# Feed-forward in two halves of its inner units, with partial sums in DRAM

## The chip, the cores and the metric

One Trainium2 chip, one core. The metric is the device time of one execution in microseconds (us). Engines are called PE (TensorE, matrix products), PEld (its weight loads), DVE (VectorE), ACT (ScalarE), POOL (GpSimd) and SP (SyncE, which here only issues DMAs).

## The reference

Sparse attention, then a mixture of experts with one expert per token, then a dense feed-forward; all results in float32.

```python
scores = scale * (q @ k.T)                        # 4 batches, 8 heads, 576 x 576, head size 64
scores = where(scores >= rowmax - tau, scores, -1e9)
x = softmax(scores) @ v                           # 2304 tokens of 512 numbers
e = argmax(normalized x @ normalized expert_emb)  # 8 experts, inner size 1024
x = gate * (relu(x @ w1[e]) @ w2[e])
h = x @ w_in                                      # 512 -> 2048
out = (h * tanh(softplus(h))) @ w_out             # 2048 -> 512
```

The feed-forward's weights w_in and w_out come as 64-bit floats (512 KB for a piece of 128x512 numbers) and have to be narrowed to 32 bits on the chip.

## The kernel before

Every matrix product of the experts and the feed-forward is made of three: both operands are split into a rounded high part (a cast on ACT) and the remainder (a subtraction on DVE or POOL), and PE multiplies high by high, high by low and low by high.

A planner (`Plan`, from line 85) holds a list of operations, each with its engine, an assumed duration, what it reads and writes, a priority and a phase, and writes out one fixed order for every engine. Buffers are rings: `Handle` objects take their places in the order of a number `at`. The numbers `PR` and `PR2` (lines 37 and 38) are the priorities' offsets. Phase 0 is everything up to the last expert; phases 1 to 15 are branches for tokens that overflow an expert's room (none run here); phase 16 is what comes after them. An engine passes the branch only when its part of phase 0 is done.

Stages: attention (to about 300 us, lines 460 to 606), experts (about 320 to 556 us), feed-forward (556 us to the end). In the experts' stage `visit` (line 987) handles one expert: SP loads four 1 MB weight chunks, each chunk is split in two halves by `weight_part` (lines 961 and 963; `PR2['split']` names, for each of the eight halves, the engine of the cast and that of the subtraction), POOL gathers the expert's tokens (line 969) and scales them (line 972), PE transposes them into a PSUM pair (line 1040), multiplies by w1 (line 1064); ACT and DVE free the PSUM pair (lines 1069 and 1070); PE multiplies by w2 (line 1087), ACT copies to `osb` (line 984) and SP stores it to `y_dram`. PSUM has three pairs of banks ("S") and two single banks ("B").

During that stage `narrow_late` (line 1232) narrows all 32 pieces of w_in and w_out: `ffn_narrow` (line 1211) loads a piece to `fraw` (two buffers), ACT scales the exponent word (line 1221), DVE does three integer operations (lines 1224, 1225, 1228), and SP stores the float32 piece to DRAM. `ffn_weights` (line 1242) loads it back later, in four chunks (c = 0 to 3, each for 4 of 16 blocks of 128 inner units), and splits it (lines 1256 and 1260). Chunks 2 and 3 use the experts' weight buffers `wh` and `wl`.

The feed-forward takes its 18 token tiles of 128 in groups of 2, 4, 4, 4, 4 (`GROUPS`). For a group `ffn_rows` (line 1262) loads the transposed rows and splits them (lines 1290 and 1292); `ffn` (line 1296) runs units of one inner block of 128 (two for the group of 2 tiles): 12 matmuls per block into a PSUM bank (line 1329), tanh and two more ACT passes (1337 to 1339), a reciprocal and a product on DVE (1343, 1344), the split of the result (ACT 1347, POOL 1348), and three matmuls for each tile into that tile's sum (line 1355), which stays in PSUM, in two pairs, over all 16 blocks. At the end of a group ACT takes each sum out (line 1361) and POOL scatters it to the output (line 1365). The first `SOON` = 5 units of the first group belong to phase 0.

## Time and profile before

| | |
|---|---|
| median of three runs (all) | 972.65 us (971.48 to 973.35) |
| the profiled execution, its span | 974.42 us, 972.7 us |
| PE busy | 912.6 us (94%) |
| DVE busy | 742.2 us (76%) |
| ACT busy | 557.7 us (57%) |
| POOL busy | 353.8 us (36%) |
| DMA | 115.47 MB, mean 119 GB/s |

The span runs from the first to the last instruction. A busy PE is one with a matmul in flight; its rate also depends on the granted clock. The stages differ much in what is busy, so the table of stages in the next section but one is the view to start from.

### The profile page before, as it was taken

The numbers are of one execution on the slowest core, as the hardware profiler recorded it, in microseconds if no ns is written. First come the engines' busy times: TensorE is split into PE (matmuls) and PEld (weight loads), VectorE is DVE, ScalarE is ACT, GpSimd is POOL, SyncE is SP. The second block draws the span as 40 slices with busy tenths as digits, with TensorE's granted clock in tenths as the row PEclk, the third lists the DMA queues.
The fourth block names the chain that finished last, engine by engine and source line by source line (L and its number), as shares of the span: only waits on it lengthen the run. The fifth ranks groups of instructions, "written<-read, shape, count | busy, mean of one in ns | idle before, by whom it ended". The sixth has DMA issues, their size and how long they took to land. (4 is left out here: it accounts for less than half of the span.)

```text
span 972.7 us, 17476 instructions
## 1 busy us (share of the span) xinstructions
PE 912.6 (94%) x6574; PEld 727.2 (75%) x6574; DVE 742.2 (76%) x1032; ACT 557.7 (57%) x916; POOL 353.8 (36%) x445
## 2 busy tenths in 40 slices
PE   5899999998989999988899998999999999999997
PEld 3556565555557899888899986888888878888885
DVE  6898988888847477967898885992958596586972
ACT  3688887787766454554566763652644445363551
POOL 4233333433223544434323732423432333333333
PEclk9899999999999999998999999999999999999999
DMA  4123433323243788989889631001010001000001
GB/s 154 60 75 103 122 104 108 96 82 112 77 153 117 286 284 303 323 255 331 301 307 325 219 113 46 23 0 44 22 42 3 22 1 44 1 1 22 22 1 44
DMA packets 45637, 115.47 MB, mean 119 GB/s; under 512 B 11029, under 2 KB 16170, under 8 KB 41450
## 3 DMA queue, kind: packets, MB, share of 16 engines
q1 hardware_dynamic: 42426, 104.03, 31.8%
q0 software_dynamic: 3120, 10.25, 3.1%
q8 instruction: 54, 0.88, 0.4%
q14 instruction: 37, 0.30, 0.1%
HBM read 91.55 MB, written 22.70 MB: 117 GB/s over the span
## 5 line engine op out<-in xcount | busy, mean ns | idle before, releaser
L1343 DVE RECIPROCAL p<-p 128x512 f32<-128x512 f32 x72 | 241.0, 3347 | 100.7 <-ACT p L1339 100.7
L1348 POOL TENSOR_TENSOR lo<-p,hi 128x512 fp32r<-128x512 f32 x72 | 93.0, 1293 | 177.4 <-ACT hi L1347 100.8
L514 PE MATMUL D<-QK 64*128 64x288 f32 (+1 forms) x640 | 109.0, 465 | 19.3 <-DVE P L521 8.3
L520 ACT ACTIVATE E<-D,m 128x576 f32<-128x576 f32 x144 | 104.1, 743 | 36.7 <-DVE m L518 31.5
L518 DVE TENSOR_REDUCE m<-D 128x1 f32<-128x576 f32 x144 | 104.7, 752 | 18.6 <-PE D L514 18.4
L521 DVE SCALAR_TENSOR_TENSOR P<-D,thr,E 128x576 f32<-128x576 f32 x128 | 101.5, 813 | 15.1 <-ACT E L520 14.2
L541 ACT COPY T<-D 128x1024 f32<-128x1024 f32 (+1 forms) x80 | 74.3, 930 | 31.5 <-PE D L538 30.8
L519 POOL TENSOR_SCALAR thr<-m,ntau 128x1 f32<-128x1 f32 x144 | 38.7, 271 | 136.0 <-DVE m L518 118.2
L572 PE MATMUL D<-T,V 128*64 128x512 f32 x320 | 84.7, 615 | 0.9 <-DVE P L521 0.5
L1347 ACT CAST hi<-p 128x512 fp32r<-128x512 f32 x72 | 43.9, 610 | 70.1 <-PE S L1355 32.2
L514 PEld LDWEIGHTS D<-QK 64*128 64x128 f32 (+1 forms) x640 | 48.5, 186 | 44.4 <-issue 19.1
L963 DVE TENSOR_TENSOR wl<-raw,wh 128x1024 fp32r<-128x1024 f32 x49 | 69.5, 1445 | 12.1 <-ACT wh L961 12.0
L1087 PE MATMUL B<-lo,wh 128*128 128x240 f32 (+6 forms) x256 | 75.6, 295 | 1.7 <-DVE lo L1070 1.7
L1087 PE MATMUL B<-hi,wh 128*128 128x240 f32 (+6 forms) x256 | 75.6, 295 | 1.1 <-ACT osb L984 1.1
L1064 PE MATMUL S<-xh,wh 128*128 128x240 f32 (+6 forms) x256 | 75.9, 296 | 0.3 <-DVE lo L1070 0.3
L1087 PE MATMUL B<-hi,wl 128*128 128x240 f32 (+6 forms) x256 | 75.3, 294 | 0.0
L1064 PE MATMUL S<-xl,wh 128*128 128x240 f32 (+6 forms) x256 | 75.2, 294 | 0.0
L1064 PE MATMUL S<-xh,wl 128*128 128x240 f32 (+6 forms) x256 | 75.1, 293 | 0.0
L963 POOL TENSOR_TENSOR wl<-raw,wh 128x1024 fp32r<-128x1024 f32 x15 | 38.1, 2541 | 84.8 <-ACT wh L961 78.3
L961 ACT CAST wh<-raw 128x1024 fp32r<-128x1024 f32 x64 | 63.4, 1050 | 2.7 <-PE B L1087 2.6
L1337 ACT ACTIVATE p<-S 128x512 f32<-128x512 f32 x36 | 21.5, 598 | 64.9 <-PE S L1329 49.8
L572 PEld LDWEIGHTS D<-TL,V 128*64 128x64 f32 x320 | 23.7, 139 | 46.2 <-issue 46.0
(298 smaller groups left out, 2340.1 us busy)
## 6 DMA issues: line engine op xcount, KB each, us to landing
raw<-in_wm_dram SPq DMA_DIRECT2D x32, 1024.0 KB
QK<-in_qk_dram SPq DMA_DIRECT2D x32, 432.0 KB
V<-in_v_dram SPq DMA_DIRECT2D x16, 512.0 KB
fraw<-in_w_in_dram SPq DMA_DIRECT2D x16, 512.0 KB
fraw<-in_w_out_dram SPq DMA_DIRECT2D x16, 512.0 KB
x_dram<-xs SPq DMA_DIRECT2D x16, 256.0 KB
w_in_dram<-c SPq DMA_DIRECT2D x16, 256.0 KB
w_out_dram<-c SPq DMA_DIRECT2D x16, 256.0 KB
```

What stands on the lines that cost most here:

```text
L514: nc.tensor.matmul(o, lhsT=QK()[r, a, q0:q0 + w], rhs=QK()[r, a, S:], start=True, stop=True)
L518: add("DVE", 680, lambda: nc.vector.tensor_reduce(m(), sv(), axis=AX.XY, op=ALU.max, negate=True), r=[sc], w=[m], prio=at + PR["max"])
L520: add("ACT", 660, lambda: nc.scalar.activation(Ev(), sv(), AF.Exp, bias=m(), scale=1.0), r=[sc, m], w=[E], prio=at + PR["exp"])
L521: add("DVE", 750, lambda: nc.vector.scalar_tensor_tensor(outs[0]().rearrange("p (a b) -> p a b", a=2), sv(), thr(), Ev(), op0=ALU.is_ge, o ...
L541: add("ACT", (2 * w + 100) / 1.2, lambda: nc.scalar.copy(T()[:, :, 0:w], pt()[:, :, 0:w]), r=[pt], w=[T], prio=at + PR["Tc"])
L572: mul = lambda j, o, c, rhs: nc.tensor.matmul(o, lhsT=V1()[:, c, :], rhs=rhs, start=(a == 0), stop=(a == 4))
L961: add("ACT", t_act(1024, False), lambda: nc.scalar.copy(hi()[:, s], raw()[:, s]), r=[kr], w=[kh], prio=prio, fill=fill)
L963: add(le, d, lambda: e.tensor_tensor(lo()[:, s], raw()[:, s], hi()[:, s].bitcast(F32), op=ALU.subtract), r=[kr, kh], w=[kl], prio=prio + . ...
L1064: hd(nc.tensor.matmul(hp(), lhsT=a()[:, kc, f], rhs=x()[:, kc, cols], start=(i == 0), stop=(i == 11)))
L1087: nc.tensor.matmul(o()[:, 0:N_], lhsT=w[a]()[:, u % 4, 128 * d:128 * (d + 1)], rhs=H2[x], start=(u == 0 and i == 0), stop=(u == 7 and i == 2))
L1343: v.reciprocal(q_(), q_())
L1348: add("POOL", t_pool(512), lambda q_=q_, gh=gh, gl=gl: g.tensor_tensor(gl(), q_(), gh().bitcast(F32), op=ALU.subtract), r=[q_, gh], w=[gl] ...
```

## The change

The feed-forward goes through its inner units in two halves. Ten sequences `sq` run: groups 0 to 4 with blocks 0 to 7, then groups 4 to 0 with blocks 8 to 15. The first half's sums are doubled on ACT and stored to a DRAM tensor `part` (18 x 128 x 512); in the second half they are loaded back, and DVE adds them while it takes the sums out of PSUM. The group in the middle keeps its rows; every other group loads and splits its rows again. Groups are 3, 4, 4, 4, 3 tiles; a unit is one block; `SOON` is 4. Rows of sequences 1 and 3 lie in the experts' weight buffers.

Of the 32 weight pieces 20 (`16 + EXTRA`) are narrowed in the experts' stage as before. The other twelve, chunk 2 of w_out and chunk 3 of both, are narrowed in the feed-forward's first half, split from there straight into their place (`direct`), and make no trip through DRAM. Narrowing works in place: the first DVE operation is a shift by a constant that overwrites the loaded words, and the last overwrites ACT's result; the buffers `c` go, and there are four of `b`.

Besides, the half `split[5]` (chunk 2, second half) of the experts' weights is subtracted on DVE instead of POOL, the second expert's tokens are scaled on ACT, the planner assumes longer DMA times (y stores 6000 for 2000 ns, expert weights 7500 for 2000, and others), and most numbers of `PR` and `PR2` are different, those of attention too.

```diff
-GROUPS = (2, 4, 4, 4, 4)
-SOON = 5
+GROUPS = (3, 4, 4, 4, 3)
+SOON = 4
+EXTRA = 4
-PR2 = {... 'split': (['ACT', 'DVE'], ['ACT', 'POOL'], ['ACT', 'DVE'], ['ACT', 'DVE'], ['ACT', 'DVE'], ['ACT', 'POOL'], ['ACT', 'DVE'], ['ACT', 'DVE']), 'sl': 28000, ... 'n1': 0.6, ...}
+PR2 = {... 'split': (('ACT', 'DVE'), ('ACT', 'POOL'), ('ACT', 'DVE'), ('ACT', 'DVE'), ('ACT', 'DVE'), ('ACT', 'DVE'), ('ACT', 'DVE'), ('ACT', 'DVE')), 'sl': 2000, ... 'n1': 0.48, ... 'dx': 15.1, 'dp': 278.01, 'd_pool': (0, 1, 2, 3), ...}
...
+        self.part = dr.tile([18, 128, 512], F32, name="part")
...
-            self.fetch(self.ids[:, j:j + 1], self.x_dram[:, :], need, xg, -600 + T + 10 * k, "POOL" if v else "ACT")
+            self.fetch(self.ids[:, j:j + 1], self.x_dram[:, :], need, xg, -600 + T + 10 * k, "POOL" if v > 1 else "ACT")
...
-            v.tensor_tensor(w(), words(U32, 0), self.by29.to_broadcast([128, 512]), op=ALU.logical_shift_right)
-            v.scalar_tensor_tensor(w(), words(U32, 1), 0x80000000, w(), op0=ALU.bitwise_and, op1=ALU.bitwise_or)
-        add("DVE", 690, lambda: v.scalar_tensor_tensor(w(), e().bitcast(U32), 3, w(), op0=ALU.logical_shift_left, op1=ALU.bitwise_or), r=[ke], w=[kw], prio=at)
+        add("DVE", 560, lambda: v.tensor_scalar(words(U32, 0), words(U32, 0), 29, None, op0=ALU.logical_shift_right), r=[kr], w=[kt], prio=at)
+        add("DVE", 690, lambda: v.scalar_tensor_tensor(words(U32, 0), words(U32, 1), 0x80000000, words(U32, 0), op0=ALU.bitwise_and, op1=ALU.bitwise_or), r=[kr, kt], w=[kt], prio=at)
+        add("DVE", 690, lambda: v.scalar_tensor_tensor(e().bitcast(U32), e().bitcast(U32), 3, words(U32, 0), op0=ALU.logical_shift_left, op1=ALU.bitwise_or), r=[kt, ke], w=[ke], prio=at)
...
-        for x, (n, i) in enumerate(self.pieces):
+        for x, (n, i) in enumerate(self.pieces[:16 + EXTRA]):
...
+            x = self.pieces.index((n, 4 * c + q))
+            direct = x >= 16 + EXTRA and self.io[n].dtype != F32
+            self.pl.phase = 0 if c < 2 else OVER + 1
+            if direct:
+                z = x - 16
+                bt = 501 + 100 * z / 16 + R["dx"]
+                raw, e = h("f", "fraw", [128, 2 * YW], F32, 2, bt), h("f", "b", [128, 512], F32, 4, bt)
+                self.ffn_narrow(n, 4 * c + q, bt + R["dp"], lambda dt, raw=raw: raw()[:, 0:1024].bitcast(dt), e, [raw, e], store=False)
+                add("ACT", t_act(512, False), lambda s=s, e=e: nc.scalar.copy(hi()[:, s], e()), r=[e], w=[(th, q)], prio=bt + R["dp"])
+                eng, dur, d = ("POOL", t_pool(512), g) if q in R["d_pool"] else ("DVE", t_dve(512), v)
+                add(eng, dur, lambda s=s, e=e, d=d: d.tensor_tensor(lo()[:, s], e(), hi()[:, s].bitcast(F32), op=ALU.subtract), r=[e, (th, q)], w=[(tl, q)], prio=bt + R["dp"])
+                continue
...
-        have = [("y", -1, k) for k in range(2)] + [("y", v, d) for v in range(2 if gi == 0 else NE) for d in range(4)]
+        have = [("y", -1, k) for k in range(2)] + [("y", v, d) for v in range(3 if sq == 0 else NE) for d in range(4)]
...
+        nu, u0 = 8 // fw, half * 8 // fw
...
+            if not half:
+                add("ACT", t_act(512), lambda ob=ob, t=t: ad(t, nc.scalar.mul(ob()[:, 0:512], acc(t), 2.0)), r=[ak(t)], w=[ob], prio=at + R["ob"])
+                add("SP", 600, lambda ob=ob, t=t: nc.sync.dma_start(self.part[t0 + t], ob()[:, 0:512]), r=[ob], w=[("part", t0 + t)], prio=at, lat=4500, dma=262e3)
+                continue
+            pt = self.row("q32", at + 12 + t)
+            add("SP", 600, lambda pt=pt, t=t: nc.sync.dma_start(pt()[:, 0:512], self.part[t0 + t]), r=[("part", t0 + t)], w=[pt], prio=at + R["fy"] + 5 + t, lat=4500, dma=262e3)
+            add("DVE", t_dve(512), lambda ob=ob, t=t, pt=pt: ad(t, v.scalar_tensor_tensor(ob()[:, 0:512], acc(t), 2.0, pt()[:, 0:512], op0=ALU.mult, op1=ALU.add)), r=[ak(t), pt], w=[ob], prio=at + R["ob"])
...
+        for sq in range(2 * G):
+            half, gi = sq // G, min(sq, 2 * G - 1 - sq)
+            self.pl.phase = OVER + 1 if sq else 0
+            if sq != G:
+                rows = self.ffn_rows(gi, sq)
+            self.ffn(gi, half, sq, rows)
```

## Rows read from the trace of the kernel before

**Rows 1.** Table of stages: stretch, busy us of each engine (instructions), clock, DMA, GB/s
```profile
core 0: us, PE busy (x) PEld busy (x) DVE busy (x) ACT busy (x) POOL busy (x), PEclk, DMA share, GB/s
0.00:300.00 300.00, 272.10 (x3009) 166.52 (x3010) 240.78 (x588) 221.78 (x339) 102.78 (x256) 0.98 0.31 105
352.00:450.00 98.00, 89.42 (x544) 87.65 (x544) 81.24 (x101) 50.15 (x83) 38.79 (x22) 0.97 0.90 300
450.00:556.60 106.60, 100.47 (x861) 99.42 (x861) 91.54 (x112) 66.20 (x125) 45.08 (x24) 0.98 0.86 294
556.60:610.30 53.70, 46.88 (x278) 39.47 (x278) 38.49 (x25) 27.44 (x48) 16.91 (x13) 0.97 0.27 82
610.30:966.10 355.80, 355.36 (x1549) 290.10 (x1547) 255.38 (x130) 167.68 (x283) 120.97 (x113) 1.00 0.06 18
```

**Rows 2.** Waits of PE, 352.0 to 556.6: total us, times, longest us
```profile
PE S L1040 <- issue: 7.2, 4, 4.3
PE S L1040 <- POOL wl L963: 4.4, 2, 2.4
```

**Rows 3.** Timeline of PE: start, us, what [idle before it <- releaser]
```profile
402.44 1.06 PE L1040 MATMUL S<-ident,q 128*128 128x128 f32 x8 [1.36 <-issue]
...
440.47 1.94 PE L1040 MATMUL S<-ident,q 128*128 128x128 f32 x8 [4.33 <-issue]
...
471.91 1.07 PE L1040 MATMUL S<-ident,q 128*128 128x128 f32 x8 [2.44 <-POOL wl L963]
...
496.43 1.06 PE L1040 MATMUL S<-ident,q 128*128 128x128 f32 x8 [1.98 <-POOL wl L963]
```

**Rows 4.** Timeline of DVE, 425 to 445
```profile
436.45 2.83 DVE L1224 TENSOR_TENSOR c<-fraw,by 128x512 uint32<-128x512 uint32 x1
...
439.92 0.45 DVE L1070 SCALAR_TENSOR_TENSOR lo<-S,hi 128x288 fp32r<-128x288 f32 x1
```

**Rows 5.** All narrowing operations by line: count, then ns least/median/most, first and last start
```profile
L1224 DVE TENSOR_TENSOR c<-fraw,by x32: 674/684/2829, 345.2 to 526.9; 128x512 uint32<-128x512 uint32 x32
L1225 DVE SCALAR_TENSOR_TENSOR c<-fraw,c x32: 691/693/2783, 346.3 to 527.6; 128x512 uint32<-128x512 uint32 x32
```

**Rows 6.** Timeline of POOL, 395 to 530
```profile
397.78 2.50 POOL L963 TENSOR_TENSOR wl<-raw,wh 128x1024 fp32r<-128x1024 f32 x1 [6.54 <-DMA raw<-in_wm_dram]
...
435.88 2.85 POOL L963 TENSOR_TENSOR wl<-raw,wh 128x1024 fp32r<-128x1024 f32 x1 [5.20 <-ACT wh L961]
...
468.22 2.73 POOL L963 TENSOR_TENSOR wl<-raw,wh 128x1024 fp32r<-128x1024 f32 x1 [5.19 <-ACT wh L961]
...
492.86 2.60 POOL L963 TENSOR_TENSOR wl<-raw,wh 128x1024 fp32r<-128x1024 f32 x1 [3.80 <-ACT wh L961]
```

**Rows 7.** Stretches, line 1224 alone: DVE busy us (instructions), clock, DMA, GB/s
```profile
352.00:450.00 98.00, 13.79 (x17) 0.97 0.90 300
450.00:530.00 80.00, 12.60 (x13) 0.98 0.90 312
```

**Rows 8.** The page's costliest groups: count | busy us, mean ns | idle before, releaser
```profile
L963 DVE TENSOR_TENSOR wl<-raw,wh 128x1024 fp32r<-128x1024 f32 x49 | 69.5, 1445 | 12.1 <-ACT wh L961 12.0
...
L963 POOL TENSOR_TENSOR wl<-raw,wh 128x1024 fp32r<-128x1024 f32 x15 | 38.1, 2541 | 84.8 <-ACT wh L961 78.3
```

**Rows 9.** Groups by line in the feed-forward, 610.3 to 966.1, columns as above
```profile
L1343 DVE RECIPROCAL p<-p 128x512 f32<-128x512 f32 x65 | 217.5, 3347 | 86.6 <-ACT p L1339 86.6
L1348 POOL TENSOR_TENSOR lo<-p,hi 128x512 fp32r<-128x512 f32 x66 | 85.3, 1294 | 163.9 <-ACT hi L1347 90.1 <-PE S L1355 47.2 <-PE B L1329 11.3
...
L1344 DVE SCALAR_TENSOR_TENSOR p<-p,B 128x512 f32<-128x512 f32 x33 | 22.7, 687 | 1.2
```

**Rows 10.** The chain that ended last: start, us, what
```profile
592.34 3.12 PE S L1329 x24
...
610.46 5.53 PE B L1329 x24
...
966.12 0.61 ACT p L1361
```

**Rows 11.** One seam between groups, columns as in rows 1
```profile
780.00:810.00 30.00, 29.79 (x131) 24.04 (x130) 21.59 (x12) 11.73 (x21) 10.73 (x12) 1.00 0.05 18
```

**Rows 12.** Timeline of DVE, 595 to 605
```profile
601.65 1.62 DVE L1292 TENSOR_TENSOR lo<-fraw,hi 128x512 fp32r<-128x512 f32 x1
603.19 0.68 DVE L1292 TENSOR_TENSOR c<-fraw,b 128x512 fp32r<-128x512 f32 x1
```

More of the change, by code (lines that the diff above doesn't have):

```diff
@@ L1171, in overflow @@
         X, H = h("p32"), [h("p32", 1 + a) for a in range(2)]
-        R = [h("b", 0), h("b", 1), h("c", 0), h("c", 1)]
+        R = [h("b", x) for x in range(4)]
         xg, xp, o, y = h("q32"), h("S"), h("B"), h("osb")
@@ L1285, in ffn_rows, with ffn @@
         for z in range(2):
-            add("SP", 600, lambda z=z: nc.sync.dma_start(raw[z]()[:, 0:2 * w].rearrange("p (x n) -> p x n", x=2), self.y_dram[2 * z:2 * z + 2, :, c0:c0 + w].rearrange("x p n -> p x n")), r=have, w=[raw[z]], prio=at + R["fy"] + z, lat=2000, dma=1024.0 * w)
+            add("SP", 600, lambda z=z: nc.sync.dma_start(raw[z]()[:, 0:2 * w].rearrange("p (x n) -> p x n", x=2), self.y_dram[2 * z:2 * z + 2, :, c0:c0 + w].rearrange("x p n -> p x n")), r=have, w=[raw[z]], prio=at + R["fy"] + z, lat=4500 if sq else 2000, dma=1024.0 * w)
         out = []
         for kc in range(4):
-            hi, lo = (lambda t=t: t().bitcast(F32R)[:, 0:w] for t in X[kc])
+            hi, lo = (lambda i=i, kc=kc: view(i, kc) for i in range(2))
             add("ACT", t_act(w, False), lambda hi=hi, kc=kc: nc.scalar.copy(hi(), part(kc)), r=[raw[kc // 2]], w=[X[kc][0]], prio=at + R["fx"] + kc)
-            eng, dur, e = ("POOL", t_pool(w), g) if gi > 1 or gi and kc % 2 else ("DVE", t_dve(w), v)
+            eng, dur, e = ("POOL", t_pool(w), g) if sq > 1 or sq and kc % 2 else ("DVE", t_dve(w), v)
             add(eng, dur, lambda hi=hi, lo=lo, kc=kc, e=e: e.tensor_tensor(lo(), part(kc), hi().bitcast(F32), op=ALU.subtract), r=[raw[kc // 2], X[kc][0]], w=[X[kc][1]], prio=at + R["fx"] + kc)
             out.append((hi, lo))
-        return X, out, ids
-    def ffn(self, gi, rows):
+        return X, out
+    def ffn(self, gi, half, sq, rows):
         nc, add, h = self.nc, self.pl.add, self.h
@@ L1301, in ffn @@
         fw, w = 4 // nt, 128 * nt
-        at = 500 + 40 * gi
-        Xk, X, ids = rows
-        idu = h("f", "fiu", [128, 4], U32, 2, at + 50)
-        place = lambda u: 409 + .1 * u if gi == 0 and u < SOON else at + 2 * u * fw
-        accs = [self.big(place(R["acc"] + x / 8)) for x in range(nt // 2)]
+        at = 500 + 20 * sq
+        last = sq == 2 * len(GROUPS) - 1
+        Xk, X = rows
+        if half:
+            ids = h("f", "fid", [128, 4], F32, 3, at)
+            add("SP", 600, lambda: nc.sync.dma_start(ids()[:, 0:nt], self.id_dram[128 * t0:128 * (t0 + nt), :].rearrange("(t p) o -> p (t o)", p=128)), w=[ids], prio=at + R["fy"] + 4, lat=2000, dma=20e3, after=[self.last_id])
+            idu = h("f", "fiu", [128, 4], U32, 2, at + 25)
+        nu, u0 = 8 // fw, half * 8 // fw
+        place = lambda u: 409 + .1 * u if sq == 0 and u < SOON else at + 2 * u * fw
+        accs = [self.big(place((R["acc"] if sq else 3.6) + x / 8)) for x in range((nt + 1) // 2)]
         acc = lambda t: accs[t // 2]()[:, t % 2, :]
@@ L1309, in ffn @@
         ad = lambda t, ins: self.of_bank(*ak(t), ins)
-        for u in range(16 // fw):
-            self.pl.phase = 0 if gi == 0 and u < SOON else OVER + 1
-            au, pu = place(u), at + 2.5 * u * fw
+        for x in range(nu):
+            u = u0 + x
+            self.pl.phase = 0 if sq == 0 and x < SOON else OVER + 1
+            au, pu = place(x), at + 2.5 * x * fw
             if u % 4 == 0:
@@ L1354, in mm2 @@
                         for n, (a, x) in enumerate(((gh, wh), (gh, wl), (gl, wh))):
-                            ad(t, nc.tensor.matmul(acc(t), lhsT=a()[:, k], rhs=x, start=(u == 0 and f == 0 and n == 0), stop=(u == 16 // fw - 1 and f == fw - 1 and n == 2)))
-                late = gi == len(GROUPS) - 1 and u >= 16 // fw - 4
+                            ad(t, nc.tensor.matmul(acc(t), lhsT=a()[:, k], rhs=x, start=(u == u0 and f == 0 and n == 0), stop=(u == u0 + nu - 1 and f == fw - 1 and n == 2)))
+                late = last and x >= nu // 2
                 add("PE", 3 * fw * 227, mm2, r=[gh, gl] + keys("w_out"), w=[ak(t)], prio=at + 1100 + 10 * t + .1 * u if late else pu + R["lag"] + .1 * t)
@@ L1414, in feed_forward @@
                 self.ffn_weights(n, c, (400 if c > 1 else 480) + 2 * c + x, tags[2 * c + x])
[L1415 to L1418 removed]
+        G = len(GROUPS)
+        for sq in range(2 * G):
[4 more added lines that the diff above has]
+            self.ffn(gi, half, sq, rows)
     def finish(self):
```

80 lines of the change are left out of this document (38 added, 42 removed).

## The prediction

> **What bounds the kernel now.** I read the stage table first [rows 1]: idle time of TensorE (PE) is the stretch minus its busy time. The feed-forward from 610.30 to 966.10 us leaves 355.80 - 355.36 = 0.4 us of idle PE at full clock: no other engine holds it there. The experts from 352.00 to 556.60 lose (98.00 - 89.42) + (106.60 - 100.47) = 14.7 us, and the granted clock of 0.97 and 0.98 costs about 2.9 + 2.1 = 5.0 us more. The entry into the feed-forward, 556.60 to 610.30, loses 6.8 us and 1.6 us of clock. Attention loses 27.9 us before 300. So what this change can win lies in about 28 us (14.7 + 5.0 + 6.8 + 1.6).
>
> Next, PE's waits in the experts [rows 2]: 7.2 and 4.4 us of 14.7 end at line 1040, the transposes of an expert's gathered rows. The table names POOL or nobody as releaser, so I put the queues side by side at one place. PE's transposes start at 440.47, after 4.33 us of nothing [rows 3]. They need a PSUM pair, which line 1070 frees on VectorE (DVE); there it ends at 439.92 + 0.45 = 440.37, and ahead of it lies a narrowing operation (line 1224) of 2.83 us [rows 4]. The same form has a median of 0.684 us [rows 5]. During just that stretch POOL runs a 2.85 us piece of line 963 [rows 6]. Such a POOL piece, of 2.50 to 2.85 us, starts 3.5 to 4.7 us ahead of each of the four transposes that end a long stop (402.44, 440.47, 471.91, 496.43), and each is its expert's second POOL piece, the one of weight chunk 2. The experts' cause is thus DVE, 83% and 86% busy, stretched by POOL at a bad moment; that the DMA engines are 0.90 and 0.86 busy is the second suspect.
>
> The Trainium skill (GPSIMD Engine Reference, 1. Specifications) says that POOL shares its SBUF interfaces with VectorE and contends with DVE instructions that have two SBUF inputs. The trace agrees, 2.83 us beside 0.684 [rows 4, 5].
>
> **The change, part by part.** Sums are made against the profiled execution's own 974.4 us (span 972.7 and 1.7 around it); the median of the three runs lies 1.8 us lower, and I take that off at the end.
>
> *Experts.* (a) Twelve of 32 narrowings leave: each is three DVE operations; line 1224 takes 13.79 us for 17 before 450 and 12.60 for 13 after it [rows 7], 26.39/30 = 0.88 each, so I take 2.6 us a piece: 31 us of DVE. (b) 12 x (0.5 + 0.25 + 0.25) MB of transfers become 12 x 0.5 MB, and those move to the feed-forward. (c) The POOL piece of chunk 2 goes to DVE: eight pieces of 2.54 us leave POOL, DVE gets eight of at most 1.45 [rows 8], 12 us. It is the piece of every PE stop above. DVE so falls by 19 us net. But pieces run as their buffers allow, 17 of 30 in the first of the two parts; the remaining 20 can fill that part as before, so (a) helps after 450 and (c) everywhere. Without (c)'s collision each of the four stops shortens by up to 2.83 - 0.68 = 2.1 us: 8.6. The clock, which was lost beside these stops, gives back most of its 5.0: I take 3.5. Of the other waits after 450, where 31 us of DVE work thin out, I take 2. Together -14. Bounds: -19 (all of 19.7 but a little) and -4 (half of the 8.2 lost after 450, nothing before). -14 is nearer to what the four pairs of rows show in common.
>
> *Entry.* Before, 16 weight pieces of chunks 2 and 3 are split beside the first units; now they aren't. But the first group has three tiles, and only four units of it can run before the overflow's branch. A unit of 384 columns asks 12 + 9 matmuls of PE and 384/512 of a gate of DVE, 0.75 x (3.35 + 0.69) = 3.0 us [rows 9]; where only the nine second matmuls (2.1 us) are left, DVE sets the pace and PE loses 1 us a unit, three times, and the fill after the branch stays. I take -2, bounds -6 and +4.
>
> *Feed-forward, PE.* The columns are the same: 192 x 2304 for the first product, 48 matmuls per tile for the second. A 512-column matmul takes 5.53/24 = 0.230 us; 24 of 256 columns take 3.12, 0.130 each, above half of it [rows 10]. A 256-column group less can only help: 0, bounds -2 and 0.
>
> *Feed-forward, DVE in the first half.* 24 full gates of 3.347 + 0.687 and 16 of three quarters: 97 + 48 = 145 us; twelve narrowings at 2.6: 31; small splits 2: 178 us, beside PE's half, (192 x 0.130 + 1632 x 0.230)/2 = 200 us [rows 10]. It fits at 89%, where the stage before has 255.38/355.80 = 72%. PE holds four PSUM banks of finished first products, some 11 us of slack of order. Cost +2; bounds 0 and +18 (rival 3).
>
> *Feed-forward, other engines.* Four groups of rows are loaded and split again: 16 casts on ACT and 16 POOL pieces of 1.29 us [rows 9], 21 us on a POOL that is 121 of 356 us busy. Twelve raw loads and 36 tile transfers of 0.25 MB in 400 us lie on a DMA system that is 0.06 busy. On SP's queue these stand in front of later row loads: a raw load waits for one of two raw buffers, and rows, partial sums and token numbers behind it wait too. Rows are asked for about half a group ahead, and a group lasts 8 units of 4.2 to 5.5 us, 33 to 44 us, so nothing. If that cover goes, a late row load stops PE for its landing and split.
>
> *Nine seams instead of four, one of them without new rows.* A seam now costs 30.00 - 29.79 = 0.2 us [rows 11]. In the second half its sums leave PSUM on DVE, behind a reciprocal of 3.35 us, where ACT took 0.61 [rows 10]; the new group's second products wait for that behind first products already in four banks. +2, bounds 0 and +8.
>
> *Tail.* The last eviction is 0.69 on DVE instead of 0.61 on ACT: +0.1, bounds -1 and +2. *Attention.* Its priorities change, its work does not: 0, bounds -4 and +4 of 27.9 idle.
>
> Sum: -14 - 2 + 0 + 2 + 0 + 2 + 0 + 0 = -12; 974.4 - 12 = 962.4; less 1.8 gives 960.6: I say 961.
>
> **The rivals.** *1, all the cover holds:* the experts give 19, the entry 6, DVE and seams cost 1: 974.4 - 24 - 1.8 = 948.6. For it: every long stop has the same moved POOL piece. Against: DVE before 450 keeps as many narrowings, and the other POOL piece (chunk 0) still meets them. Chance 0.20.
>
> *2, the change doesn't do what it says:* the experts wait for DMA and gathers, 20 narrowings keep the part before 450 as dense, and DVE gets the POOL pieces in addition. The experts give 4, the entry 1, the rest costs 4: 974.4 - 1 - 1.8 = 971.6. For it: DMA at 0.90. Against: PE starts again 0.1 us after line 1070 ends [rows 3, 4], not after a landing. Chance 0.14.
>
> *3, slower:* DVE becomes the bound of the first half. Each of a piece's three operations has two SBUF inputs or may otherwise meet POOL's piece of 1.29 us, which runs once a unit; line 1292 on DVE shows it in this stage, 1.62 us where the next is 0.68 [rows 12]. If all wait, a piece costs 3 x (0.68 + 1.29) = 5.9 us, twelve 71, and DVE needs 147 + 71 = 218 us against 200: +18. It decides from (200 - 147)/12 = 4.4 us a piece. With -14, -2 and +2: 974.4 + 4 - 1.8 = 976.6, and more where seams cost more. Against: POOL is a third busy, so on average a piece pays about one collision. Chance 0.17.
>
> By the skill's rule above, rival 3 is what every overlap of a two-input narrowing with POOL would give; the trace has such overlaps, but shows in [rows 5] that most narrowings escape them. A second page (VectorE: DVE Perf Modes, Mode 2x_2P) says that an fp32 operation with one tensor source in SBUF can run at two results a cycle; the new shift by a constant would then take half of 0.684, an estimate of 4 us less DVE in the first half, and rival 3 would need dearer collisions. No row here shows it.
>
> **How the numbers follow.** Forecast 961 with 0.49 (its own range 953 to 968), rivals 0.20, 0.14, 0.17. 0.2% is 1.9 us, about what a measurement here can tell. Faster: 0.49 + 0.20 + 0.05 of rival 2 = 0.74; same: 0.08 of it; slower: rival 3 and the last 0.01, 0.18. The range 946 to 977 takes in rivals 1 and 2 with attention's bounds of 4 on either side of the forecast and leaves out half of rival 3 and the edge of 1, under 0.2.
>
> **What would show it.** Right: PE idle in the experts' 200 us falls from 14.7 to about 4; no narrowing there above 1 us at an expert's transposes; the last expert ends some 14 us earlier, if attention ends at the same time; the feed-forward from its first matmul to its last stays within 4 us of 409.4 (966.1 - 556.7), less the entry's gain. Rival 1: it gets shorter. Rival 2: stops at line 1040 stay before 450. Rival 3: PE waits for line 1344 or 1348 in the first half, and narrowing lines mean 1.3 us or more. The prediction is wrong also if PE waits at seams for the new DVE eviction, or for rows that come late on SP's queue.

## The result and the profile after

The changed kernel takes 948.4 us (median of 4 runs, 948.07 to 948.67), the one before 972.25: a ratio of 0.9754, with an interval of 0.9737 to 0.9771. That is 23.85 us less, where 11.7 were forecast: inside the range of 946 to 977, but twice the gain, and in size rival 1 (948.6, given 0.20). A later series of both kernels gave 19.1 us (e6 below).

The profiled executions (974.42 and 948.07 us of their own) differ by 26.35. By PE's marks, the first w1 product of the second expert, the last product of the last expert and the last matmul of all, the difference falls like this:

| stage | before | after | difference | forecast |
|---|---|---|---|---|
| up to the second expert | 352.1 | 345.9 | -6.2 | 0 |
| second to last expert | 204.4 | 184.2 | -20.2 | -14 |
| feed-forward, to the last matmul | 409.5 | 408.6 | -0.9 | +2 |
| from there to the end of the span | 6.7 | 7.7 | +1.0 | +0.1 |

First the table of stages of the kernel after, columns as in [rows 1]. Its second and third stretch are the experts, cut where the fifth expert's first product starts; the next is the entry into the feed-forward, and the last its rest.

```profile
0.00:300.00 300.00, 273.19 (x3031) 167.83 (x3032) 244.73 (x604) 225.45 (x344) 103.45 (x255) 0.98 0.32 105
345.90:442.50 96.60, 95.57 (x618) 95.30 (x617) 70.44 (x98) 52.02 (x86) 36.46 (x22) 1.00 0.85 295
442.50:530.10 87.60, 87.60 (x785) 87.60 (x784) 61.70 (x84) 54.47 (x103) 26.14 (x14) 1.00 0.68 234
530.10:570.60 40.50, 36.23 (x166) 30.22 (x166) 26.17 (x20) 19.34 (x40) 12.01 (x10) 0.96 0.28 83
570.60:938.70 368.10, 367.82 (x1663) 306.74 (x1661) 298.20 (x200) 200.48 (x360) 155.31 (x146) 1.00 0.22 70
```

The kernel before, cut in the same way:

```profile
352.10:459.90 107.80, 99.22 (x619) 97.45 (x619) 88.09 (x110) 54.15 (x90) 43.31 (x25) 0.97 0.90 301
459.90:556.50 96.60, 90.47 (x785) 89.42 (x784) 84.51 (x103) 62.00 (x118) 40.51 (x21) 0.98 0.85 292
```

In the experts PE's idle time fell from 8.6 + 6.1 = 14.7 us to 1.0, and the granted clock is 1.00 (its upper level, 2.4 GHz) throughout. The first of the two parts gave 11.2 us, the second 9.0. DVE's busy time fell from 172.6 to 132.1 us there, by 40.5 us, where the prediction had 19. The clock of the kernel before is below 1.00 in three stretches of 5 us there, which make 0.49 x 5 + 0.19 x 5 + 0.34 x 5 = 5.1 us; the first two begin where PE's longest stop ends, at 440.47 [rows 3].

```profile
440.00:445.00 5.00, 4.00 (x17) 3.66 (x18) 5.00 (x10) 1.85 (x3) 2.08 (x3) 0.51 0.92 315
445.00:450.00 5.00, 5.00 (x33) 5.00 (x33) 3.29 (x5) 3.06 (x5) 2.45 (x2) 0.81 0.96 357
525.00:530.00 5.00, 5.00 (x32) 5.00 (x31) 4.58 (x6) 1.89 (x4) 0.00 (x0) 0.66 0.93 307
```

The one stop left is the whole answer to the question of PE's waits, 345.9 to 530.2, which answers to [rows 2]:

```profile
PE S L1040 <- issue: 1.0, 1, 1.0
```

The feed-forward shows what the prediction left to it. Behind the entry PE idles for 368.10 - 367.82 = 0.3 us, against 0.4 before [rows 1], with DVE 81% busy in place of 72%. The second products follow each other, start to start, in 0.232 us in the mean where it was 0.230; for 864 of them that is 1.7 us.

The narrowing operations of the kernel after, by line (count, ns least/median/most, first and last start), answer to [rows 5]:

```profile
L1224 DVE TENSOR_SCALAR fraw<-fraw x32: 417/422/958, 334.6 to 747.8; 128x512 uint32<-128x512 uint32 x32
L1225 DVE SCALAR_TENSOR_TENSOR fraw<-fraw x32: 679/691/2559, 335.1 to 751.2; 128x512 uint32<-128x512 uint32 x32
L1226 DVE SCALAR_TENSOR_TENSOR b<-b,fraw x32: 680/692/1511, 336.0 to 752.0; 128x512 uint32<-128x512 uint32 x32
```

Line 1225 still has an operation of 2.56 us: the collisions with POOL are fewer, not gone. One of 2.41 us stands right at an expert's transposes, beside a POOL piece (timelines of DVE, POOL and PE), and the stop behind it is the 1.03 us shown above:

```profile
423.73 2.41 DVE L1225 SCALAR_TENSOR_TENSOR fraw<-fraw 128x512 uint32<-128x512 uint32 x1
423.16 2.43 POOL L963 TENSOR_TENSOR wl<-raw,wh 128x1024 fp32r<-128x1024 f32 x1 [15.64 <-ACT wh L961]
427.39 0.63 PE L1040 MATMUL S<-ident,q 128*128 128x128 f32 x4 [1.03 <-issue]
```

The shift by a constant takes 0.422 us where the old first operation took 0.684. A subtraction of 128x1024 takes 1.218 us in the median in the kernel before (line below, columns as in [rows 5]), so 512 columns more cost 0.534, and 0.150 of the 0.684 don't depend on the length. Half of 0.534 and the 0.150 give an estimated 0.417; the prediction's half of 0.684 had halved the fixed part too. The Trainium skill (VectorE: DVE Perf Modes, Mode 2x_2P) has two results a cycle for an operation with one tensor source in SBUF. The trace agrees, with 0.422 beside the 0.417.

```profile
L963 DVE TENSOR_TENSOR wl<-raw,wh x49: 1208/1218/3462, 306.3 to 539.6; 128x1024 fp32r<-128x1024 f32 x49
```

And the split of the experts' weights on DVE (the page's costliest groups, as [rows 8]) has eight operations more and takes 0.9 us less in sum, since their mean fell from 1445 to 1238 ns:

```profile
L963 DVE TENSOR_TENSOR wl<-raw,wh 128x1024 fp32r<-128x1024 f32 x57 | 68.6, 1238 | 26.0 <-ACT wh L961 25.2
```

### The profile page after: what moved, and what is told of

Same layout as the page of the kernel before. It is cut to its first block, busy times and chain, and to the rows that moved or that the text cites. A ratio compares the mean times of both kernels' runs of the same rounds, so it can differ in the third digit from the quotient of the medians.

```text
span 946.4 us, 17660 instructions
## 1 busy us (share of the span) xinstructions
PE 904.3 (96%) x6574; PEld 728.2 (77%) x6574; DVE 730.6 (77%) x1068; ACT 574.0 (61%) x967; POOL 355.2 (38%) x463
## 5 line engine op out<-in xcount | busy, mean ns | idle before, releaser
L1363 DVE RECIPROCAL p<-p 128x512 f32<-128x512 f32 (+1 forms) x80 | 242.1, 3026 | 72.4 <-ACT p L1359 72.4
L1368 POOL TENSOR_TENSOR lo<-p,hi 128x512 fp32r<-128x512 f32 (+1 forms) x80 | 95.8, 1199 | 173.0 <-ACT hi L1367 109.3
L514 PE MATMUL D<-QK 64*128 64x288 f32 (+1 forms) x640 | 106.8, 458 | 19.1 <-DVE P L521 9.0
L1367 ACT CAST hi<-p 128x512 fp32r<-128x512 f32 (+1 forms) x80 | 45.6, 570 | 77.3 <-DVE p L1364 76.4
L541 ACT COPY T<-D 128x1024 f32<-128x1024 f32 (+1 forms) x80 | 74.3, 930 | 27.4 <-PE D L538 26.6
L963 DVE TENSOR_TENSOR wl<-raw,wh 128x1024 fp32r<-128x1024 f32 x57 | 68.6, 1238 | 26.0 <-ACT wh L961 25.2
L1357 ACT ACTIVATE p<-S 128x512 f32<-128x512 f32 (+1 forms) x40 | 22.2, 555 | 56.8 <-PE S L1348 53.9
L1375 PE MATMUL S<-wh,hi 128*128 128x512 f32 x144 | 56.5, 392 | 0.0
```

What stands on the lines that cost most here:

```text
L514: nc.tensor.matmul(o, lhsT=QK()[r, a, q0:q0 + w], rhs=QK()[r, a, S:], start=True, stop=True)
L541: add("ACT", (2 * w + 100) / 1.2, lambda: nc.scalar.copy(T()[:, :, 0:w], pt()[:, :, 0:w]), r=[pt], w=[T], prio=at + PR["Tc"])
L1363: v.reciprocal(q_(), q_())
L1368: add("POOL", t_pool(fw * w), lambda q_=q_, ghw=ghw, glw=glw: g.tensor_tensor(glw(), q_(), ghw().bitcast(F32), op=ALU.subtract), r=[qt, gh ...
L1375: ad(t, nc.tensor.matmul(acc(t), lhsT=a()[:, k], rhs=x, start=(u == u0 and f == 0 and n == 0), stop=(u == u0 + nu - 1 and f == fw - 1 and ...
```

## The experiments

On the chips of these runs the kernel before varies from 964 to 974 us, with medians of 969.3 to 970.9; ratios are to the runs of the same series. "First" and "second part" are the two parts of the experts' stage as cut above (107.8 and 96.6 us before, 96.6 and 87.6 after), "start" is the first w1 product of the second expert (352.1 and 345.9).

**Both kernels once more.** e5 is the kernel before, e6 the kernel after, each with an empty line added.

> The kernel before, unchanged, for a second profile beside the others of this chip. If the long stops before 450 belong to its fixed order, they stand again at the same transposes and the experts take 204 us within 2; if they come and go from run to run, they differ by 5 us or more.

Measured: 969.89 us, ratio 0.9997 (0.9975 to 1.002); start 350.1, first part 107.1, second 97.1.

> The changed kernel, unchanged, on the same chip as the others: 948 within 2 us; experts 184 us, start of the second expert's products within 2 us of 345.9.

Measured: 950.5 us, ratio 0.979 (0.9747 to 0.9833); start 347.0, parts 96.7 and 87.5. The stage times of these two profiles repeat within 1 us in the experts, and the six stops at line 1040 are 11.6 us again in e5. Up to the second expert only 3.1 of the 6.2 us repeat. The gain of the whole is 969.63 - 950.5 = 19.1 us here.

### How many narrowings the experts' stage holds

e3 leaves all 32 in it, e16 24, e15 16 (20 in the kernel after).

```diff
-EXTRA = 4
+EXTRA = 16      # e3;  8 in e16,  0 in e15
```

> The changed kernel, with all 32 weight pieces narrowed in the experts' stage and stored to DRAM (EXTRA = 16), none in the feed-forward. Theory C: experts within 4 us of 184, total 946 to 953, as the feed-forward's first half has 27 us less on DVE. Theory L: the part after 450 fills again, experts 194 or more, total 957 or more. Theory O: within 2 us of 948.

Measured: 982.4 us, ratio 1.0147 (1.0105 to 1.0188), slower than the kernel before. The first part stays at 96.6 (with 14 narrowings in it, as in the kernel after), the second is 97.1, with 14 narrowings and PE's products waiting for DVE (PE's waits, 446.3 to 543.4, behind the table):

```profile
349.70:446.30 96.60, 95.56 (x618) 95.29 (x617) 70.16 (x98) 51.90 (x86) 37.11 (x22) 1.00 0.85 295
446.30:543.40 97.10, 92.30 (x785) 91.22 (x784) 80.91 (x111) 58.42 (x109) 24.56 (x14) 0.96 0.83 288
```

```profile
PE B L1087 <- DVE lo L1070: 4.7, 4, 1.8
```

Then PE stands at the first matmul of the feed-forward, until ACT casts the first group's rows (timeline of PE):

```profile
550.87 0.69 PE L1348 MATMUL S<-hi,raw 128*128 128x384 f32 x1 [7.15 <-ACT hi L1303]
```

The feed-forward as a whole takes 428.1 us instead of 408.6, and only part of the 19.5 us is this stop. The changed kernel without the move thus loses. Theory L was right on the second part.

> The changed kernel with 24 narrowings in the experts' stage and 8 in the feed-forward. Theory L: 90.8 us behind the fifth expert's start instead of 87.6, total 953 to 955. Rival K: 87 to 88 us, total 950 to 951.

Measured: 965.97 us, ratio 0.9954 (0.9929 to 0.998). Both theories missed: the first part is 96.7, the second 96.9, and the feed-forward is 6.6 us longer. DVE is no fuller in the second part than in the first of this kernel (69.82 of 96.90 and 70.00 of 96.70):

```profile
347.80:444.50 96.70, 95.66 (x619) 95.39 (x619) 70.00 (x98) 51.91 (x86) 37.26 (x22) 1.00 0.84 294
444.50:541.40 96.90, 90.33 (x785) 89.95 (x784) 69.82 (x96) 57.34 (x107) 24.96 (x14) 0.96 0.71 244
```

What stops PE is one wait of 5.45 us, at a product into a bank that ACT has to empty (line 984); for DVE it waits 1.1 us there. The clock of 0.96 costs 3 to 4 us more. The timeline of ACT shows why ACT is late: in front of that copy stands the cast of a narrowed piece that is being loaded back (line 1268), and it waits 8.18 us for its DMA.

```profile
504.40 0.35 ACT L984 COPY osb<-B 128x224 f32<-128x224 f32 x1 [0.48 <-ACT wh L961]
512.92 1.91 ACT L1268 CAST raw<-raw 128x512 fp32r<-128x512 f32 x3 [8.18 <-DMA raw<-w_in_dram]
514.74 0.34 ACT L984 COPY osb<-B 128x224 f32<-128x224 f32 x1
```

The timeline of PE, at the same place:

```profile
515.13 0.55 PE L1087 MATMUL B<-hi,wh 128*128 128x224 f32 x1 [5.45 <-ACT osb L984]
```

> The changed kernel with 16 narrowings in the experts' stage and 16 in the feed-forward. Theory L for the part behind the fifth expert: 0.79 us for each narrowing ((97.1 - 87.6)/12), so 84.4 us there instead of 87.6 and a total of 947, as the feed-forward hides the four more. Rival K (at 20 nothing of that stage waits for DVE any more; the rest is PE's own work): 87 to 88 us, total 950; more if the feed-forward's start then waits for its weights.

Measured: 949.84 us, ratio 0.9786 (0.9738 to 0.9834); parts 96.6 and 87.6. Rival K holds: with 20 narrowings nothing in the second part waits any more, and four fewer bring nothing. PE's wait for DVE there is thus 4.7 us with 32 (e3), 1.1 with 24 and none with 20 and 16. In the table, columns as before, PE is busy for the whole of it:

```profile
444.40:532.00 87.60, 87.60 (x785) 87.60 (x784) 54.36 (x72) 52.54 (x99) 23.90 (x14) 1.00 0.60 207
```

**DVE's work or the transfers?** In the kernel before, e9 leaves the three DVE operations of the last 12 narrowings out and keeps their loads and stores; e10 leaves those transfers out and keeps the work of ACT and DVE, on other data.

```diff
+        dve = w is not e                      # e9: w is e for x >= 20
+        if dve:
         add("DVE", 690 + 690, low, ...)
...
-        add("SP", 600, lambda: nc.sync.dma_start(raw(src.dtype), src[:, s]), ...)
+        if own:                               # e10: not for x >= 20; the same for the store
+            add("SP", 600, lambda: nc.sync.dma_start(raw(src.dtype), src[:, s]), ...)
```

> The kernel before, with the three DVE narrowing operations of the last twelve pieces left out; their loads, ACT's pass and their stores stay. Theory V (the twelve pieces cost the part after 450 by DVE's time): that part, from the fifth expert's products (459.9) to the last expert's end (556.5), falls from 96.6 to 90 us or less, total 962 or less. Theory D (by their transfers): within 2 us of 96.6, total 968 to 972.

Measured: 965.25 us, ratio 0.9926 (0.9903 to 0.9949).

```profile
350.30:455.50 105.20, 98.83 (x618) 97.28 (x618) 85.85 (x107) 54.26 (x90) 44.86 (x25) 0.97 0.92 310
455.50:545.30 89.80, 88.27 (x785) 87.74 (x784) 60.11 (x69) 62.36 (x117) 39.34 (x21) 1.00 0.89 312
```

> The kernel before, with the loads and stores of the last twelve pieces left out; ACT and DVE do the same operations on other data, and the feed-forward loads other pieces in their place. Theory D: the part from the fifth expert falls from 96.6 to 90 us or less, total 962 or less. Theory V: within 3 us of 96.6, total 966 to 972.

Measured: 974.74 us, ratio 1.0043 (1.0018 to 1.0068); parts 109.5 and 97.6, with the DMA share in the second down from 0.85 to 0.59. So the second part's gain is DVE's: with its 36 operations gone the part gets shorter by 6.8 of the 9.0 us at a DMA share of 0.89, and without the transfers not at all. The second suspect of the prediction falls there; for the first part e17 below has 97.0 us at a DMA share of 0.90.

**What the moved narrowings cost in the feed-forward.** e11 is the kernel after without the DVE operations of the 12 direct pieces.

```diff
         kt = (kr, "t")
+        if not store:
+            return
         add("DVE", 560, lambda: v.tensor_scalar(...))
```

> The changed kernel, with the three DVE operations of the twelve pieces in the feed-forward left out; their loads, ACT's pass and the split stay. If these 23 us of DVE (12 x 1.9) are hidden behind PE: the feed-forward stays at 408.5 within 1 us, total 947 to 951. If DVE is near its bound there, as I priced with +2 (at most +18): 406 or less, total 2 to 18 us lower.

Measured: 952.4 us, ratio 0.9793 (0.9766 to 0.982); e6 had 0.979. The feed-forward takes 410.5 us, 2 more than after. There is no gain, so they cost nothing there.

### The weight piece and the narrowing in place

e1 moves the piece alone to DVE, in the kernel before; e2 takes it back to POOL in the kernel after.

```diff
-'split': (..., ['ACT', 'POOL'], ['ACT', 'DVE'], ['ACT', 'DVE'])
+'split': (..., ['ACT', 'DVE'], ['ACT', 'DVE'], ['ACT', 'DVE'])      # e1; the reverse in e2
```

> The kernel before, with only the second half of weight chunk 2 subtracted on DVE instead of POOL. Theory C (each long stop of PE in the experts comes from a narrowing operation on DVE that is stretched by that POOL piece): the experts, 352 to 556.6, shrink by 8 to 12 us, total about 962. Theory L (the stage suffers from the sheer number of narrowings on DVE): DVE gets 10 us more work in the stage, so no gain or up to 5 us slower, 972 to 977. Theory O (the planner's new order, priorities and DMA times make the gain): within 2 us of before, 970 to 974.

Measured: 970.69 us, ratio 0.9999 (0.9974 to 1.0023). The profiled run, the fastest of its ten with 965.4, has a first part of 99.4, 8.4 us less, and of PE's six stops at line 1040, 11.6 us [rows 2], two are left (PE's waits in 351.7 to 546.7; the first of them, 2.5 us, is the first part's):

```profile
PE B L1087 <- DVE lo L1070: 4.7, 6, 1.4
PE S L1040 <- issue: 2.9, 2, 2.5
PE S L1064 <- DVE lo L1070: 0.4, 1, 0.4
```

But in the second part the products of line 1087 now wait 4.7 us for DVE. In the kernel before, in 352.1 to 556.5, they waited less:

```profile
PE B L1087 <- DVE lo L1070: 1.7, 4, 0.8
```

So in the second part the stops at line 1040 fell from 4.4 to 0.4 us and the waits for DVE rose from 1.7 to 5.1: the loss moved, and the part is at 95.6. The experts of this profile, 195.0 us, are what theory C gave, but in the median nothing is left. Where the slower runs lose it isn't shown, since no profile of one was taken.

> The changed kernel, with that one piece given back to POOL. Theory C: the stops return at the transposes, experts 184 to about 194 us, total about 958. Theory L: DVE is relieved by 10 us, total within 2 us of 948. Theory O: within 2 us of 948.

Measured: 956.01 us, ratio 0.9863 (0.9835 to 0.989). The experts are as after (96.8 and 88.0), though their narrowings again reach 2651 and 2910 ns; of the 5.5 us by which it is behind e6, most is lost ahead of them, where the start moves from 345.9 (e6: 347.0) to 350.8. So the collision is there, and in the new order, with 12 narrowings gone, it doesn't cost the experts anything. None of the three theories gave both this and the total.

e7 narrows in place in the kernel before; e12 takes both back in the kernel after, the piece to POOL and the first operation to its two-input form.

```diff
-            v.tensor_tensor(w(), words(U32, 0), self.by29.to_broadcast([128, 512]), op=ALU.logical_shift_right)
...
+        add("DVE", 560, lambda: v.tensor_scalar(words(U32, 0), words(U32, 0), 29, None, op0=ALU.logical_shift_right), r=[kr], w=[kt], prio=at)   # e7; the reverse in e12
```

> The kernel before, with narrowing in place alone (shift by a constant over the loaded words, buffers c not used): the first of three DVE operations falls from 0.68 to 0.42 us and no longer meets POOL. Theory N (stretched narrowings make the stops, and it is enough that one of three can't be stretched): experts shorter by 5 to 10 us, total 960 to 966. Theory L (the number of pieces in the stage): DVE saves 32 x 0.26 = 8 us of 173, total within 3 us of before, 968 to 972. Theory O (order and assumed times): within 2 us of before.

Measured: 971.46 us, ratio 1.0016 (0.9992 to 1.004). The profiled run, the fastest of its ten, has parts of 101.9 and 102.4: the first gives 5.9, the second takes 5.8 back, with 13 narrowings in it instead of 11. Theory N misses. The shift meets POOL as its forerunner did (columns as in [rows 5]; below it, one place in the timelines of DVE and POOL):

```profile
L1224 DVE TENSOR_SCALAR fraw<-fraw x32: 411/428/2667, 340.9 to 531.7; 128x512 uint32<-128x512 uint32 x32
```

```profile
418.68 2.67 DVE L1224 TENSOR_SCALAR fraw<-fraw 128x512 uint32<-128x512 uint32 x1
418.48 2.58 POOL L963 TENSOR_TENSOR wl<-raw,wh 128x1024 fp32r<-128x1024 f32 x1 [8.63 <-ACT wh L961]
```

All five shifts above 2 us start 0.1 to 0.4 us after such a POOL piece has started, and end 0.29 us after it ends.

> The changed kernel, with the POOL piece of chunk 2 given back and the first narrowing operation again one of two SBUF inputs (0.68 us, a tensor_tensor with a constant tile, still in place). Theory C with redundancy (the collision makes the stops, and either of the two edits alone is enough to avoid them): the part from the second expert's products to the fifth's grows from 96.6 to 102 us or more, total 958 or more. Theory O (the order of the changed kernel avoids the stops, whatever collides): it stays within 2 us of 96.6, and the total within 3 us of the kernel with the piece alone given back, 956.

Measured: 954.79 us, ratio 0.9814 (0.9786 to 0.9842); start 350.7, parts 97.8 and 88.3, with DVE busy for 80.44 us in the first. Theory O holds. Against e2 (0.9863) the dearer shift costs nothing that shows.

### The planner's numbers

e8 gives the kernel before the new assumed DMA times, `f0`, `n1`, `np` and `sl`, and the second expert's gathers on ACT. e13 takes the assumed times back in the kernel after; e14 takes all of these back. e4 takes back attention's priorities alone.

```diff
-... w=[kr], prio=at - 4, lat=2000, ...      # and four more lines of this kind
+... w=[kr], prio=at - 4, lat=8500, ...      # e8; the reverse in e13 and e14
-'f0': (100, 127, 152, 153), 'n1': 0.6, 'np': 390.59, 'sl': 28000
+'f0': (122, 132, 44, 187), 'n1': 0.48, 'np': 416.51, 'sl': 2000      # e8; the reverse in e14
-PR = {'er': -12.15, ...}
+PR = {'er': -25.44, ...}      # e4, all of PR
```

> The kernel before, with the planner's numbers that bear on the experts alone: assumed DMA times (y stores 6000 ns, expert weights 4000 and 7500, narrowing 8500 and 8000, feed-forward weights 4500), f0, n1, np, sl, and the second expert's tokens scaled on ACT. No operation is added or removed. Theory O: the stops before 450 go, experts 190 to 196 us, total 958 to 964. Theories C, L and N: within 3 us of before, 968 to 973.

Measured: 992.61 us, ratio 1.0198 (1.0144 to 1.0252), the slowest of all, which no theory gave; start 358.8, parts 103.2 and 106.4. The first part is shorter than before, with 14 narrowings in it, but stops for 4.9 us stay at its transposes; the second is 9.8 us longer, with DVE busy for 96.84 us of it. The assumed times do what they say: ACT, which in the first part of the kernel before stood at narrowing loads for 22.1 us, here does so for 1.9 (its waits there, by kind; before first).

```profile
ACT b L1221 <- DMA fraw<-in_w_out_dram: 14.5, 7, 5.5
ACT b L1221 <- DMA fraw<-in_w_in_dram: 7.6, 4, 3.3
```

```profile
ACT b L1221 <- DMA fraw<-in_w_in_dram: 1.2, 1, 1.2
ACT b L1221 <- DMA fraw<-in_w_out_dram: 0.7, 1, 0.7
```

PE's stops, from the second expert's start to the last expert's end (358.8 to 568.4), stay:

```profile
PE S L1040 <- issue: 7.7, 4, 2.8
PE B L1087 <- DVE lo L1070: 5.0, 6, 2.0
PE S L1040 <- POOL q L972: 2.8, 1, 2.8
```

> The changed kernel with the assumed DMA times of the kernel before (2000 ns everywhere that the change had raised them); work and all priorities stay. Theory O (the order written by the planner, of which these times are one input, removes PE's stops ahead of 450): from the second to the fifth expert's first product 102 to 108 us instead of 96.7, stops of 2 us and more at the transposes of gathered rows return, total 955 to 962. Theory L (20 narrowings instead of 32 do it, whatever the order): 96 to 98 us there, no stop over 1.5 us, total 949 to 952.

Measured: 956.45 us, ratio 0.9855 (0.9807 to 0.9903); start 349.4, parts 98.7 and 89.5. One stop of 2.43 us is back ahead of the fifth expert. Each theory has its share: the first part is between them, and the total is what O gave.

> The changed kernel with the old assumed DMA times and also the old numbers f0, n1, np and sl and the second expert's gathers back on POOL: with that, of the experts' order, only the attention's numbers, the split and the count of narrowings are new. Theory O: 104 to 108 us from the second to the fifth expert's first product, total 957 to 965. Theory L: 96 to 98 us, total 949 to 952. If e13 is as the changed kernel and this one is slow, the times don't matter and the numbers do.

Measured: 954.98 us, ratio 0.9825 (0.9765 to 0.9886), with runs of 951.13, 951.64, 958.32 and 962.14. The profiled run is the last of these; 17.1 us at half clock from 340.9 on (the lower level, 1.2 GHz) explain some 8.5 us of it. Parts 100.0 and 87.6. The first part loses 3.4 us, where theory O wanted 7 to 11.

> The changed kernel, with attention's priorities (PR) of the kernel before. If the 6 us by which the experts' main part starts earlier (345.9 against 352.1) come from attention's new order: the start goes back to about 352 and the total to 954 or 955. If they come from the experts' priorities (PR2, the first expert's casts), or are only the spread of one profile: total within 2 us of 948.

Measured: 960.04 us, ratio 0.9909 (0.9875 to 0.9942). The last score is at 271.4 as after (271.6), so the new priorities win nothing up to there; 4.7 us are lost from there to the start (350.4). The parts are 99.3 and 88.4, but the first holds 24 products of line 1087 (2.7 us) more than after, which PE did ahead of the start there, and its idle time is 1.0 us as after. So some 7 us are lost ahead of the experts' main part and little in it.

### The edits together

e17 gives the kernel before the three edits of e1, e7 and 20 narrowings, with the feed-forward in one pass. e18 undoes in the kernel after what e4, e12 and e14 undo, all at once; in-place narrowing, the halves and the moved pieces stay.

```diff
-        for x, (n, i) in enumerate(self.pieces):
+        for x, (n, i) in enumerate(self.pieces[:20]):      # e17, with the diffs of e1 and e7
...
+            j = 4 * c + q if self.pieces.index((n, 4 * c + q)) < 20 else (4 * c + q) % 8
```

> The kernel before with three of the change's edits in the experts' stage together: the weight piece of chunk 2's second half on DVE, narrowing in place, and only 20 narrowings. The other twelve are left out altogether (their places in the feed-forward are filled with copies of the first ones), the feed-forward stays in one pass. Theory N (fewer narrowings are what the stage needs, and with room there the two small edits show their gain): second to fifth expert 97 to 100 us, behind it 88 to 90, total 949 to 956. Rival P (the order that the change's numbers write is needed as well): stops of together 5 us and more stay before the fifth expert, 104 to 108 us there, total 960 to 966.

Measured: 951.83 us, ratio 0.9823 (0.9783 to 0.9864). Start 348.3, experts 184.5:

```profile
348.30:445.30 97.00, 95.26 (x619) 94.99 (x618) 75.84 (x110) 54.43 (x89) 35.76 (x22) 1.00 0.90 318
445.30:532.80 87.50, 87.50 (x786) 87.50 (x785) 54.62 (x73) 56.13 (x105) 27.22 (x17) 1.00 0.68 230
```

Theory N holds. In the medians the piece alone gave 0.1 us, narrowing in place nothing, DVE's part of the twelve narrowings 5.5 (e9) and their transfers nothing (e10); the three edits together give 17.4. The kernel before with 20 whole narrowings and neither small edit was not run; e18 comes nearest. The first part is at 97.0 with DMA 0.90 busy, the old priorities, and 18 narrowings in it, where the kernel before has 19 and the one after 14 (the counts are those of line 1224 in each part). Its narrowings cost 7.85 + 13.74 + 14.56 = 36.2 us for 18, or 2.01 each, where before they cost 15.16 + 15.99 + 15.57 = 46.7 for 19, or 2.46.

> The changed kernel with all of its edits ahead of the feed-forward undone but one: old priorities of attention, old assumed DMA times and numbers f0, n1, np and sl, the weight piece back on POOL, the two-input shift (still in place). What is left is the feed-forward in two halves and the twelve narrowings moved there. Theory N: the second part of the experts stays at 88 to 90 us, the first at 97 to 102; with what the single undone edits cost (some 6 for the piece, 10 for attention's numbers, less where they overlap) a total of 955 to 966. Rival P: the first part goes back to 104 to 108 us, total 967 and more.

Measured: 959.36 us, ratio 0.9895 (0.9866 to 0.9924); start 350.7.

```profile
350.70:453.40 102.70, 97.49 (x619) 96.42 (x619) 85.22 (x104) 53.36 (x88) 46.17 (x25) 0.98 0.86 298
453.40:540.80 87.40, 87.40 (x784) 87.40 (x784) 56.61 (x72) 53.44 (x100) 33.39 (x18) 1.00 0.61 212
```

Theory N holds in the total; the first part is 0.7 us above its range. The second part keeps its gain by the count alone. Of the first part's 11 us about half is left, and one stop of 3.7 us stands again at the transposes. DVE has 85.22 us of work there, near the 88.09 of the kernel before. With 20 narrowings the experts thus give 14.3 us without the moved piece, the shift by a constant and the new order, 19.9 with the first two (e17), 18.3 with the new order alone (e12, table below) and 20.2 with all.

```profile
350.70:448.50 97.80, 95.51 (x618) 94.88 (x618) 80.44 (x98) 52.49 (x87) 47.11 (x25) 1.00 0.83 294
448.50:536.80 88.30, 87.99 (x785) 87.64 (x784) 64.16 (x77) 54.93 (x102) 35.84 (x18) 1.00 0.68 228
```

## Why the prediction came out as it did

*What bounds the kernel.* Right: it was DVE in the experts, not the transfers (e9, e10, e17). The 14.7 us of idle time and the 5 us of clock that stood at risk there were the right sum, and 18.7 of the 19.7 us came back. The lost clock came back with the stops.

*Experts, -14 forecast, -20.2 measured: the step that failed.* The sum took back only 14.1 of the 19.7 us: 8.6 at the stops, 3.5 of clock, 2 of other waits. Measured, PE's stops at line 1040 fell by 10.6 us (11.6 to 1.0), the clock gave 5.1, the other waits 3.1, all there were, and the products themselves took 1.4 less, for which there was no term and for which no run shows a cause. The bound of -19 was passed.

The reason for taking less was that "the remaining 20 can fill that part as before, so (a) helps after 450 and (c) everywhere". That failed. The first part holds 14 narrowings where it held 19, and e3, with all 32 in the stage, holds 14 there too: this is the new order's work (17 with the old assumed times, e13). In the old order 18 stayed (e17), and the part was as short. DVE's relief, put at 19 us, was 40.5: the narrowings in the two parts took 77.1 us before and 38.8 after, 38.3 less instead of 31, and the eight pieces taken from POOL, put at 12 us more, cost nothing. Line 963 took 57.7 us on DVE there before and 55.5 after, since its other pieces got faster: with the piece alone moved (e1) the mean fell from 1445 to 1271 ns.

The collision, the term's main mechanism, is there (e7), but it explains the stops only in part. Its 8.6 took 2.15 us from each of four stops, of which one was 1.36 us long and one 1.98. With the piece moved and all narrowings kept (e1), two stops of 2.9 us stay and waits for DVE grow. With the collision back in the changed kernel (e2) no long stop comes. Also the sign "no narrowing there above 1 us at an expert's transposes" was wrong: one of 2.41 us stands there and costs 1.03.

*Rival 1.* Its experts, 19, were nearest, and its argument against itself was no hindrance. But that its total is met is luck in part: it had 6 at the entry, where 2.5 came, and nothing ahead of the experts, where 6.2 came in the profiles and 3.1 in the repeats.

*Up to the second expert, 0 forecast, -6.2 measured.* Outside the bounds of 4 in the profiles; 3.1 us in the repeats (e5, e6). Of the 6.2 us 4.8 were won by the last score (276.4 and 271.6; 274.0 and 272.2 in the repeats), and 1.7 of these are clock: before this start PE ran at half clock for 13.6 us in the profile of before and for 10.2 in that of after. The last 1.4 lie between the last score and the start, 75.7 and 74.3 us. Taking back attention's numbers or the piece makes that stretch 79.0 (e4) and 78.4 us (e2), longer than in the kernel before, so they cost the changed kernel dearly but don't tell what it gained. Attention's new priorities win nothing up to the last score (e4 has it at 271.4 with the old ones); what they and the rest win behind it stays open.

*Entry, -2.* Idle time fell from 6.8 to 4.3 us, with 1.6 us of clock lost in both: -2.5. Right.

*DVE in the first half, +2, and rival 3.* The term is 0 (e11). DVE is busy for 158.3 of the first 184.4 us behind the entry, 86%, as the sum of 89% had it, but the narrowings there cost 5.26 + 8.73 + 8.74 = 22.7 us for twelve, 1.9 each instead of 2.6, with no more than 0.3 us of idle PE in the whole stage. Rival 3, which needed 4.4 each, falls.

*Seams, +2.* Nothing shows; the new evictions on DVE hold PE up at none of the nine seams.

*PE's columns, 0.* Some +1.7, by the second products' 0.232 us for 0.230: small, and outside the bounds of -2 to 0.

*Tail, +0.1.* +1.0, inside its bounds.

*Rival 2.* It falls with its mechanism (e10). Its idea that the edits might not do what they say holds for the two small ones alone (e1 and e7 in the median).

*What would have shown the right size.* The sum took each edit's price at one place and added. Put beside the stage's whole loss of 19.7 us, DVE's whole relief would have pointed at the upper bound. What is shown is that 20 narrowings instead of 32 carry most of it (e18), and that with them either the new order (e12) or the two small edits (e17) bring most of the rest. With all 32 each of the small edits alone brings nothing in the median. That places can't be added at all is not shown: e9 tests only DVE's part of the twelve, and in the profiles the experts' gains of e1 (9.4) and e18 (14.3) come to more than the 20.2 measured.

Why less work ends the loss is argued. DVE's share points that way: 82% and 87% busy in the two parts before, where PE lost 8.6 and 6.1 us, and 73% and 70% after, where it lost 1.0 and none. But the share alone doesn't settle it: e12 loses 2.3 us at the same 82%, e7 3.5 and e17 1.7 at 78% (all in the first part), and e16 loses at 72%, by a wait in ACT's queue. Nor does the count of narrowings in the first part: e8 still stops for 4.9 us there with 14. The order in which DVE meets its work may count too; no run isolates it.

## What to carry to other kernels

Where several edits relieve one engine that is short over a whole stage, price them together against the whole idle time and lost clock of that stage: a small one alone may give nothing in the median, as e1 and e7 did, where a stop only moves. Ask what a restructuring lets go of: here the feed-forward's halves cost nothing that shows (408.6 us where one pass took 409.5), and the twelve narrowings that they made room for won most of the time. And look at what else stands in an in-order queue ahead of the instruction that frees a buffer: one reload that came late, with four narrowings more, took back all that the second part had gained (e16).

## What the runs showed of the hardware

A shift by a constant, of one input in SBUF with a stride of two words, took 0.422 us for 128x512 where the two-input shift took 0.684. That is near the 0.417 estimated above for two results a cycle. It was stretched by POOL no less: up to 2.667 us in e7 and 2.651 in e2, where POOL has the second piece of each expert, against 0.958 after and 0.598 in e17, where it has not. In e7 each of the five above 2 us ended 0.29 us after the POOL piece that had started before it. The prediction cited the Trainium skill (GPSIMD Engine Reference, 1. Specifications) for contention of POOL with DVE's two-input instructions; that section of the Trainium skill names DVE's two-port modes as well. These rows agree for both, if the shift runs in such a mode, as its 0.422 us suggests.
